# First layer of experts 1 to 6 as seven block products in place of eight, in a chunked-attention and mixture-of-experts kernel

## The chip, the core and the metric

The kernel runs on one core of a Trainium2 chip. Five engines with instruction queues of their own work side by side: TensorE (PE: matmuls, with its weight loads shown apart as PEld), VectorE (DVE), ScalarE (ACT), GpSimd (POOL) and SyncE (SP), from which most DMAs are issued. Each engine takes its instructions strictly in the order in which they stand in its queue; engines wait for each other on semaphores. The metric is the device time of one execution in microseconds, as the median of the runs.

## What is computed

Three stages follow each other; the output of one is the input of the next.

```python
def _moe_ref(x, w_gate, w1, w2):                 # stage 1: x is the attention's output, 1536 x 512
    ...                                          # P: a softmax balanced over tokens and experts, 1536 x 8
    for e in range(E):                           # 8 experts, D = 512, F = 1024
        h = np.maximum(x @ w1[e], 0.0)           # first layer
        ye = h @ w2[e]                           # second layer
        out += P[:, e:e + 1] * ye
    return out

def reference(**kwargs):
    attn_out = _attn_ref(...)                    # 2 x 8 heads, 768 tokens, chunks of 32
    x = attn_out.transpose(0, 2, 1, 3).reshape(B * S, H * D)
    x = _moe_ref(x=x, **moe_kwargs)              # every token through every expert
    return _moe2_ref(x=x, **moe2_kwargs)         # every token through its best expert
```

All is float32. The change concerns `x @ w1[e]` of stage 1 for six of the eight experts.

## The kernel before

Matmuls take operands of 32 bits in a rounded form (F32R). To keep precision each operand is held as two parts, hi (the value rounded) and lo (the rest), and each product is three matmuls into one PSUM accumulation: hi by hi, hi by lo and lo by hi (`mm3`).

The attention's output stands transposed in SBUF as `xhi` and `xlo`: 128 partitions by 4 channel blocks (`KD`) by 1536 tokens. Stage 1 goes through 16 units (expert e, half u of the 1024 hidden columns). A unit goes through groups of four token tiles of 128 (unit 0: of two, because the attention of later tokens still runs). For each group `m1_h` makes four blocks of hidden columns: 12 matmuls of 512 tokens into a PSUM tile `ph`, then ACT writes `hh`, the ReLU rounded, and DVE writes `hl`, the rest. Then `m1_y` makes four tiles of the second layer: 12 matmuls of 512 columns into a PSUM tile `py`, which DVE multiplies by the token's weight and adds to `acc` in SBUF. `ph` and `py` have two buffers each (`ps_m`).

Weights come as chunks of 128 by 512 (256 KB) on SP's queue into four buffers `raw`. `chunk_conv` splits each: ACT casts `raw` to hi (`ah`, `bh`), POOL subtracts to get lo (`al`, `bl`). Eight chunks serve a unit; the table `convs` says after which piece of work each split stands in the program. The order written in the code isn't the order in the queues: the tile framework moves instructions ahead where their inputs allow, by a model of its own.

In unit 1 the attention's PSUM pool (`ps_a`) still serves the balancing of P (`sinkhorn_iter`), of which the steps stand between the matmuls. At its end expert 0's sums are scaled (`scale_expert0`). 36 DMAs (`fills`) that clear buffers of the last stage are taken off a list through the units. In the last unit the routing of stage 2 begins.

```python
nc.scalar.activation(hh, ps, AF.Relu)
nc.vector.scalar_tensor_tensor(hl, ps, 0.0, f32(hh), ALU.max, ALU.subtract)
```

Of the kernel before, what the change touches and what calls it, by code (L numbers as in the profile page):

```python
# [9 lines left out]
F32 = mybir.dt.float32  # L10
F32R = mybir.dt.float32r
# [9 lines left out]
P = 128  # L21
# [6 lines left out]
def f32(ap):  # L28
    return ap.bitcast(F32)
# [3 lines left out]
def kernel(  # L33
# [97 lines left out]
    SK = WN + NM  # L131
    ast = ExitStack()
# [3 lines left out]
    ps_a = ast.enter_context(tc.tile_pool(name="ps_a", bufs=4, space=PSUM))  # L136

# [197 lines left out]

    hcur = {}

    def m1_h(e, u, t0, nt, f):
        ps = ps_m.tile([P, nt * P], F32, tag="ph", name="ph")
        sl = slice(t0 * P, (t0 + nt) * P)  # L340
        fs = slice(f * P, (f + 1) * P)
        terms = []
        for kk in range(KD):
            wh, wl = wts[e, u, "a", kk]
            terms += [(wh[:, fs], xhi[:, kk, sl]), (wh[:, fs], xlo[:, kk, sl]), (wl[:, fs], xhi[:, kk, sl])]
        mm3(ps, terms)
# [391 lines left out]
    post, fills, rq = [], [], []  # L738
    e0 = None
    for nu, (e, u) in enumerate(units):  # L740
        last = nu == len(units) - 1
        gs = [(t, 2) for t in range(0, NT, 2)] if nu == 0 else [(t, GT) for t in range(0, NT, GT)]
        L = sum(NF + nt for _, nt in gs)
        convs = ([13, 15, 16, 25] if nu == 0 else [4, 7, 10, 14]) + [L - 3, L - 2]
        if nu:
            convs += [1, 2]
        if nu == 2:
            zst = ExitStack()
            zrow = zst.enter_context(tc.tile_pool(name="zp", bufs=1, side="right")).tile([P, ROW], F32, name="zrow")
# [32 lines left out]
        for t0, nt in gs:  # L782
# [7 lines left out]
            for wi, w in enumerate(work):  # L790
# [31 lines left out]
        if nu == 1:  # L822
# [110 lines left out]
```

## Time and profile before

| What | Value |
|---|---|
| median of 3 runs | 1349.53 us (1347.64 to 1350.32) |
| profiled execution | 1351.69 us, of which the span from first to last instruction is 1350.0 us |
| mean granted TensorE clock | 0.995 |
| busy in the span | PE 1320.2 us (98%), DVE 506.2, ACT 348.4, POOL 229.6 |
| matmuls | 6604 |

A page of the profile counts an engine as busy from the start of an instruction to its end. Matmuls overlap: the time of one from start to end is longer than the distance to the next, so the pace is read from the starts in the timeline and not from the mean of one. Idle time is put down to the engine that ended it.

### The profile page before, as it was taken

The page shows a single profiled execution, that of the slowest core. Times are in us where ns is not written, and L with a number is a line of the kernel's source. Part 1 is how long each engine was busy: PE and PEld are TensorE (multiplying, and loading weights), DVE is VectorE, ACT ScalarE, POOL GpSimd, SP SyncE. Part 2 cuts the span into 40 slices and gives each one's busy share as a digit, 9 for nine tenths or more (in the row PEclk, how much of TensorE's full clock was granted, in tenths as well). Part 3 has the DMA queues.
Part 4 walks back from the last instruction along what each step waited for, and adds up shares of the span by engine and source line. Part 5 has one row for each costly group of instructions (what it writes and reads, how often), then busy time and mean ns, then how long its engine had stood idle before and what let it go on. Part 6 is the DMA issues. An engine that isn't in the chain of part 4 may idle for free. (4 is left out here: it accounts for less than half of the span.)

```text
span 1350.0 us, 17171 instructions
## 1 busy us (share of the span) xinstructions
PE 1320.2 (98%) x6604; PEld 1093.7 (81%) x6604; DVE 506.2 (37%) x1021; ACT 348.4 (26%) x647; POOL 229.6 (17%) x257
## 2 busy tenths in 40 slices
PE   7999999999999999999999999999999999889997
PEld 6888788888888888888888888888888888678775
DVE  7666353222222222222222222222222234745566
ACT  4332214121202020202121111111111112444455
POOL 5221303030303030303030202021111112300001
PEclk9999999999999999999999999999999999989999
DMA  9342641020202020202020201010111001476560
GB/s 202 88 92 72 187 157 53 10 63 0 63 1 63 0 63 0 63 1 63 0 63 0 63 7 57 16 47 17 46 32 32 0 16 44 159 245 222 167 198 16
DMA packets 86960, 90.86 MB, mean 67 GB/s; under 512 B 49835, under 2 KB 49835, under 8 KB 86852
## 3 DMA queue, kind: packets, MB, share of 16 engines
q1 hardware_dynamic: 84708, 84.15, 21.4%
q0 software_dynamic: 2000, 5.34, 1.1%
q8 instruction: 56, 0.92, 0.3%
q14 instruction: 52, 0.43, 0.1%
q10 hardware_dynamic: 144, 0.03, 0.0%
HBM read 74.70 MB, written 16.03 MB: 67 GB/s over the span
## 5 line engine op out<-in xcount | busy, mean ns | idle before, releaser
L127 PE MATMUL ph<-xhi,ah 128*128 128x512 f32 (+1 forms) x816 | 309.8, 380 | 2.9 <-DVE hl L350 2.9
L127 PE MATMUL ph<-xhi,al 128*128 128x512 f32 (+1 forms) x816 | 308.1, 378 | 0.0
L127 PE MATMUL ph<-xlo,ah 128*128 128x512 f32 (+1 forms) x816 | 307.9, 377 | 0.0
L127 PE MATMUL py<-bh,hh 128*128 128x512 f32 x768 | 300.3, 391 | 0.0
L127 PE MATMUL py<-bl,hh 128*128 128x512 f32 x768 | 299.4, 390 | 0.0
L127 PE MATMUL py<-bh,hl 128*128 128x512 f32 x768 | 299.4, 390 | 0.0
L349 ACT ACTIVATE hh<-ph 128x512 fp32r<-128x512 f32 (+1 forms) x204 | 116.7, 573 | 694.7 <-PE ph L127 681.1
L350 DVE SCALAR_TENSOR_TENSOR hl<-ph,hh 128x512 fp32r<-128x512 f32 (+1 forms) x204 | 134.5, 659 | 378.3 <-ACT hh L349 378.0
L369 DVE SCALAR_TENSOR_TENSOR acc<-py,pr,acc 128x512 f32<-128x512 f32 x168 | 126.2, 751 | 300.2 <-PE py L127 297.2
L119 POOL TENSOR_TENSOR al<-raw,ah 128x512 fp32r<-128x512 f32 x64 | 82.0, 1293 | 741.1 <-ACT ah L118 689.2
L127 PEld LDWEIGHTS ph<-xhi,ah 128*128 128x128 f32 x816 | 153.8, 189 | 31.5 <-DVE hl L350 3.3
L127 PEld LDWEIGHTS ph<-xhi,al 128*128 128x128 f32 x816 | 153.7, 188 | 28.3
L127 PEld LDWEIGHTS ph<-xlo,ah 128*128 128x128 f32 x816 | 153.9, 189 | 27.9
L127 PEld LDWEIGHTS py<-bh,hl 128*128 128x128 f32 x768 | 144.2, 188 | 29.6
L127 PEld LDWEIGHTS py<-bh,hh 128*128 128x128 f32 x768 | 144.2, 188 | 29.4
L127 PEld LDWEIGHTS py<-bl,hh 128*128 128x128 f32 x768 | 144.2, 188 | 29.3
L119 POOL TENSOR_TENSOR bl<-raw,bh 128x512 fp32r<-128x512 f32 x62 | 79.5, 1309 | 53.9 <-ACT bh L118 53.9
L533 DVE TENSOR_TENSOR w<-raw,w 128x512 fp32r<-128x512 f32 x112 | 72.3, 686 | 40.0 <-ACT w L532 39.4
L579 PE MATMUL ph<-w,gx 128*128 128x512 f32 x312 | 80.2, 404 | 1.7 <-PEq L888 1.7
L596 PE MATMUL py<-w,hh 128*128 128x512 f32 x312 | 79.7, 401 | 0.0
L579 PEld LDWEIGHTS ph<-w,gx 128*128 128x128 f32 x312 | 57.9, 191 | 15.8 <-issue 2.9
L532 ACT CAST w<-raw 128x512 fp32r<-128x512 f32 x112 | 63.4, 619 | 9.6 <-DMA raw<-in_moe_w_dram 9.4
(165 smaller groups left out, 769.6 us busy)
## 6 DMA issues: line engine op xcount, KB each, us to landing
raw<-in_moe_w_dram SPq DMA_DIRECT2D x224, 256.0 KB
disp<-zrow SPq DMA_DIRECT2D x24, 257.0 KB
xg<-disp SPq DMA_DIRECT2D x19, 257.0 KB
vin<-in_v_dram SPq DMA_DIRECT2D x20, 176.0 KB
kin<-in_k_dram SPq DMA_DIRECT2D x12, 256.0 KB
qin<-in_q_dram SPq DMA_DIRECT2D x12, 256.0 KB
out_dram<-zrow SPq DMA_DIRECT2D x12, 256.0 KB
vin<-in_mem_v_dram SPq DMA_DIRECT2D x24, 16.0 KB
```

Of the source, the lines that this page charges most:

```text
L119: (eng or nc.gpsimd).tensor_tensor(lo, raw, f32(hi), ALU.subtract)
L127: nc.tensor.matmul(ps, l, r, start=(i == 0), stop=(i == n - 1))
L349: nc.scalar.activation(hh, ps, AF.Relu)
L350: nc.vector.scalar_tensor_tensor(hl, ps, 0.0, f32(hh), ALU.max, ALU.subtract)
L369: nc.vector.scalar_tensor_tensor(a, ps, pr[:, t, e:e + 1], a, ALU.mult, ALU.add)
L532: nc.scalar.copy(h, raw)
L533: nc.vector.tensor_tensor(l, raw, f32(h), ALU.subtract)
L579: nc.tensor.matmul(pss[u], *terms[n], start=(n == 0), stop=(n == len(terms) - 1))
L596: nc.tensor.matmul(py[0], *terms[n], start=(n == 0), stop=(n == len(terms) - 1))
```

## The change

For experts 1 to 6 the units go away. Tokens are cut in two halves of 768 (b=0 and b=1), channels in two halves of 256, hidden columns in two halves of 512. The product of such 2 x 2 blocks takes eight block products; the changed kernel makes seven, of sums and differences of the blocks, and adds the results (the form with 15 additions that is due to Winograd). `m1_g(e, fi, n)` does this for one of four blocks of 128 columns in each half (`fi`) and one of two pieces of 384 tokens in each half (`n`): seven times six matmuls of 384 tokens into four PSUM tiles (`sa`, `sb`, `sc`, `sd`), two of them accumulating a second product, with four additions on DVE, one on POOL and two copies on ACT to combine them through the SBUF tile `stmp`, and four ReLU pairs into slices of `hbig`. `m1_d` then makes six tiles of the second layer (6 matmuls each); they stand one `m1_g` later (`late_d`), and take `ph` and `py` in turn. Each token tile is now added to `acc` four times in an expert, before twice.

The sums of x are made once, in unit 1 (`xs_build`): three go to a new tile `tsum`, one overwrites the upper channel half of the second token half in `xhi` and `xlo`; what stood there is saved to DRAM (`xkeep`) and read back for expert 7. The sums of the weights are made for each `fi` from two chunks of `w1` (`conv_pair`): 11 instructions on POOL and 7 casts on ACT, each on 128 x 256.

```diff
     for e in range(E):
+        if 0 < e < E - 1:
+            wv = w1[e].rearrange("(k p) (u f) -> p k u f", p=P, u=NH)
+            for fi in range(NF):
+                for dh in range(2):
+                    chunks.append((e, fi, "s", dh, wv[:, dh * KH:(dh + 1) * KH, :, fi * P:(fi + 1) * P]))
+                for f in (fi, fi + NF):
+                    chunks.append((e, f // NF, "b", f % NF, w2[e, f * P:(f + 1) * P, :]))
+            continue
...
+    def conv_pair(e, fi):
+        r0, r1 = raw_view(raws.pop(done[0])), raw_view(raws.pop(done[0] + 1))
+        a11, a21, a12, a22 = r0[:, :, 0, :], r0[:, :, 1, :], r1[:, :, 0, :], r1[:, :, 1, :]
+
+        def split(name, x):
+            w = wpa.tile([P, 512], F32R, tag="wa", name="ws").rearrange("p (a k f) -> p a k f", a=2, k=KH)
+            nc.scalar.copy(w[:, 0], x)
+            nc.gpsimd.tensor_tensor(w[:, 1], x, f32(w[:, 0]), ALU.subtract)
+            wts[e, fi, name] = w
+
+        split("a11", a11)
+        split("a12", a12)
+        split("a22", a22)
+        nc.gpsimd.tensor_tensor(a22, a21, a22, ALU.add)
+        split("s1", a22)
+        nc.gpsimd.tensor_tensor(a21, a11, a21, ALU.subtract)
+        nc.gpsimd.tensor_tensor(a11, a22, a11, ALU.subtract)
+        split("s2", a11)
+        split("s3", a21)
+        nc.gpsimd.tensor_tensor(a12, a12, a11, ALU.subtract)
+
+        def rest():
+            split("s4", a12)
+            done[0] += 2
+            chunk_dma(2)
+
+        return rest
...
+        def three(kk, n):
+            (b11, b12, b21, b22), c, _ = parts(kk, n)
+            x11, x12, x22, x21 = [stmp[:, i, :] for i in range(4)]
+            for x, b in ((x11, b11), (x12, b12), (x22, b22), (x21, b21)):
+                nc.gpsimd.tensor_tensor(x, b[0], b[1], ALU.add)
+            nc.gpsimd.tensor_tensor(x11, x12, x11, ALU.subtract)
+            nc.gpsimd.tensor_tensor(x12, x22, x12, ALU.subtract)
+            nc.gpsimd.tensor_tensor(x22, x22, x11, ALU.subtract)
+            nc.gpsimd.tensor_tensor(x21, x22, x21, ALU.subtract)
+            for i, x in ((0, x22), (1, x12), (2, x21)):
+                nc.scalar.copy(tsum[:, i, 0, kk, c], x)
+                nc.vector.tensor_tensor(tsum[:, i, 1, kk, c], x, f32(tsum[:, i, 0, kk, c]), ALU.subtract)
...
+    def m1_g(e, fi, n):
...
+        def put(key, x):
+            z = hcount[1] % 8 * 2 * SN
+            hcount[1] += 1
+            hh, hl = hbig[:, z:z + SN], hbig[:, z + SN:z + 2 * SN]
+            nc.scalar.activation(hh, x, AF.Relu)
+            nc.vector.scalar_tensor_tensor(hl, x, 0.0, f32(hh), ALU.max, ALU.subtract)
+            hsum[fi, n, key] = (hh, hl)
+
+        prod(A, "a11")
+        nc.scalar.copy(s1, A)
+        prod(B_, "s2")
+        nc.vector.tensor_tensor(s1, B_, s1, ALU.add)
+        prod(C, "s1")
+        nc.scalar.copy(s5, C)
+        prod(D_, "a22")
+        prod(A, "a12", True)
+        put((0, 0), A)
+        prod(B_, "s3")
+        nc.vector.tensor_tensor(w, B_, s1, ALU.add)
+        nc.vector.tensor_tensor(c21, w, D_, ALU.subtract)
+        nc.gpsimd.tensor_tensor(s5, w, s5, ALU.add)
+        put((1, 0), c21)
+        prod(C, "s4", True)
+        nc.vector.tensor_tensor(s1, C, s1, ALU.add)
+        put((0, 1), s1)
+        put((1, 1), s5)
...
+        tag = ("py", "ph")[ycount[0] % 2]
...
+            for fi in range(NF):
+                for n in range(NQ):
+                    m1_g(e, fi, n)
+                    if n == 0:
+                        if e < E - 2 or fi < NF - 1:
+                            conv(1)
+                        else:
+                            conv(2)
+                    flush_d()
+                    late_d.append((e, fi, n))
+                    conv(1)
...
+            xq = {2: three[0], 5: three[1], 8: three[2], 11: three[3], 14: one[0], 16: one[1], 18: one[2], 20: one[3]}
```

The first place where the queues differ is ACT at the end of unit 0. Before, after the last cast of the attention (`xhi`), come the ReLU of the unit's last token groups (`hh`, 128 x 256) and the first casts of unit 1's chunks, none of them waiting for POOL:

```order
L285 CAST xhi<-xps 128x4x128 [waits PE_49]
L349 ACTIVATE hh<-ph 128x256 [waits PE_49] x3
L349 ACTIVATE hh<-ph 128x256 [waits PE_49,Activation_49]
L118 CAST ah<-raw 128x512 [waits DMAHW6_49,PE_49]
L118 CAST ah<-raw 128x512 [waits DMAHW7_49,PE_49]
L349 ACTIVATE hh<-ph 128x256 [waits DVE_49,PE_49]
```

Now the casts of `xs_build`, which is written in unit 1, stand there too (`tsum`, each waiting for POOL):

```order
L449 CAST tsum<-stmp 128x384 [waits Pool_49] x5
L405 ACTIVATE hbig<-ph 128x256 [waits PE_49] x2
L449 CAST tsum<-stmp 128x384 [waits Pool_49] x3
L405 ACTIVATE hbig<-ph 128x256 [waits PE_49]
L145 CAST ah<-raw 128x512 [waits PE_49]
L405 ACTIVATE hbig<-ph 128x256 [waits PE_49]
L449 CAST tsum<-stmp 128x384 [waits Pool_49] x3
L145 CAST bh<-raw 128x512 [waits PE_49]
L157 CAST ws<-raw 128x256 [waits DMAHW2_49,DMAHW1_49]
```

What moved: six casts (one more stands ahead of the five shown) that wait for POOL's sums are ahead of the first two of the last four ReLU of unit 0, three more ahead of the third, and three more, with the first casts of a weight pair, ahead of unit 1's first ReLU. POOL's queue at that place, from the first sum on, holds the 32 sums of `three` with no ReLU's work between them.

The second place is ACT in the middle of stage 1. Before, in a unit, 11 ReLU follow each other, and the eight casts of weights stand in one place:

```order
L349 ACTIVATE hh<-ph 128x512 [waits DVE_49,PE_49] x11
L118 CAST ah<-raw 128x512 [waits DMAHW4_49,PE_49]
L118 CAST ah<-raw 128x512 [waits DMAHW5_49,PE_49]
L349 ACTIVATE hh<-ph 128x512 [waits DVE_49,PE_49]
L118 CAST ah<-raw 128x512 [waits DMAHW0_49,Pool_49]
```

Now, in one `m1_g` of every two, the seven casts of the next weight pair (`ws`) are mixed with the copies out of PSUM (`stmp`) and the four ReLU (`hbig`):

```order
L497 COPY stmp<-sa 128x384 [waits DVE_49,PE_49]
L157 CAST ws<-raw 128x256 [waits DMAHW5_49,DMAHW4_49]
L157 CAST ws<-raw 128x256 [waits DMAHW7_49,DMAHW6_49,PE_49]
L501 COPY stmp<-sc 128x384 [waits PE_49]
L157 CAST ws<-raw 128x256
L157 CAST ws<-raw 128x256 [waits PE_49,Pool_49]
L492 ACTIVATE hbig<-sa 128x384 [waits PE_49]
L157 CAST ws<-raw 128x256 [waits Pool_49]
L157 CAST ws<-raw 128x256 [waits PE_49]
L157 CAST ws<-raw 128x256 [waits PE_49,Pool_49]
L492 ACTIVATE hbig<-stmp 128x384 [waits DVE_49]
L492 ACTIVATE hbig<-stmp 128x384 [waits Pool_49]
```

What moved: three of the casts wait for sums that POOL makes in the same stretch, and ReLU stand behind them.

The third place is POOL in that same stretch. Before, its queue held nothing but the subtractions of eight chunks in a unit. Now it holds two of them (`bl`), then ten instructions of a weight pair, and behind these the sum `stmp<-stmp` (L508) of the running `m1_g`, of which the ReLU is the last row above:

```order
L146 TENSOR_TENSOR bl<-raw,bh 128x512 [waits DMAHW1_49,Activation_49]
L146 TENSOR_TENSOR bl<-raw,bh 128x512 [waits DMAHW6_49,Activation_49]
L158 TENSOR_TENSOR ws<-raw,ws 128x256 [waits DMAHW2_49,DMAHW3_49,PE_49,Activation_49]
L158 TENSOR_TENSOR ws<-raw,ws 128x256 [waits DMAHW5_49,DMAHW4_49,Activation_49]
L158 TENSOR_TENSOR ws<-raw,ws 128x256 [waits PE_49,Activation_49]
L164 TENSOR_TENSOR raw<-raw 128x2x128 [waits Pool_49]
L166 TENSOR_TENSOR raw<-raw 128x2x128 [waits Pool_49]
L167 TENSOR_TENSOR raw<-raw 128x2x128 [waits Pool_49]
L158 TENSOR_TENSOR ws<-raw,ws 128x256 [waits Activation_49]
L170 TENSOR_TENSOR raw<-raw 128x2x128 [waits Pool_49]
L158 TENSOR_TENSOR ws<-raw,ws 128x256 [waits PE_49,Activation_49]
L158 TENSOR_TENSOR ws<-raw,ws 128x256 [waits Activation_49]
```

The next row in that queue is L508. What moved: a sum that the second layer needs stands behind twelve instructions that it doesn't need.

## Rows read from the trace of the kernel before

**Rows 1.** The page: span, and busy time of each engine.

```profile
span 1350.0 us, 17171 instructions
PE 1320.2 (98%) x6604; PEld 1093.7 (81%) x6604; DVE 506.2 (37%) x1021; ACT 348.4 (26%) x647; POOL 229.6 (17%) x257
```

**Rows 2.** Windows: busy time of each engine in a unit, then at unit 1's start.

```profile
core 0: us, PE busy (x) PEld busy (x) DVE busy (x) ACT busy (x) POOL busy (x), PEclk, DMA share, GB/s
280.00:345.00 65.00, 65.00 (x289) 53.81 (x288) 17.31 (x24) 12.04 (x20) 10.17 (x8) 1.00 0.11 33
...
166.00:172.00 6.00, 4.43 (x12) 3.42 (x13) 2.55 (x8) 1.65 (x4) 1.74 (x2) 0.72 0.93 295
```

**Rows 3.** Waits of PE from 100 to 1040 us, all of them.

```profile
PE ph L127 <- DVE hl L350: 2.9, 1, 2.9
PE lps L296 <- DVE lt L293: 0.4, 1, 0.4
```

**Rows 4.** Timeline of PE, matmuls of 512: first and 49th of a row of them.

```profile
405.68 0.39 PE L127 MATMUL ph<-xhi,ah 128*128 128x512 f32 x1
...
416.56 0.39 PE L127 MATMUL py<-bh,hh 128*128 128x512 f32 x1
```

**Rows 5.** Timeline of PE, matmuls of 256: first of 22, and what follows them.

```profile
88.10 0.29 PE L127 MATMUL ph<-xhi,al 128*128 128x256 f32 x1
...
90.73 0.40 PE L127 MATMUL py<-bh,hh 128*128 128x512 f32 x1
```

**Rows 6.** Groups by line and form: count, busy us, mean ns, idle before.

```profile
L127 PEld LDWEIGHTS ph<-xhi,ah 128*128 128x128 f32 x816 | 153.8, 189 | 31.5 <-DVE hl L350 3.3
...
L369 DVE SCALAR_TENSOR_TENSOR acc<-py,pr,acc 128x512 f32<-128x512 f32 x168 | 126.2, 751 | 300.2 <-PE py L127 297.2 <-PE lp L441 1.5 <-PE lp L443 1.4
L350 DVE SCALAR_TENSOR_TENSOR hl<-ph,hh 128x512 fp32r<-128x512 f32 x180 | 124.4, 691 | 365.7 <-ACT hh L349 365.6
L349 ACT ACTIVATE hh<-ph 128x512 fp32r<-128x512 f32 x180 | 107.5, 598 | 664.2 <-PE ph L127 650.6 <-PE lp L443 11.2 <-PE cp L473 2.3
L119 POOL TENSOR_TENSOR al<-raw,ah 128x512 fp32r<-128x512 f32 x64 | 82.0, 1293 | 741.1 <-ACT ah L118 689.2 <-PE ph L127 51.9
...
L254 POOL TENSOR_TENSOR es<-es,sm 128x384 f32<-128x384 f32 x24 | 19.8, 827 | 45.5 <-DVE sm L253 41.3 <-DMA vin<-in_v_dram 3.8 <-ACT xhi L285 0.4
...
L350 DVE SCALAR_TENSOR_TENSOR hl<-ph,hh 128x256 fp32r<-128x256 f32 x24 | 10.1, 421 | 12.6 <-ACT hh L349 12.4
...
L349 ACT ACTIVATE hh<-ph 128x256 fp32r<-128x256 f32 x24 | 9.2, 384 | 30.6 <-PE ph L127 30.5
...
L333 ACT ACTIVATE acc<-acc,pr 128x512 f32<-128x512 f32 x12 | 8.1, 719 | 2.6 <-DVE pr L330 1.4 <-DVE acc L367 1.2
...
L430 POOL TENSOR_TENSOR osum<-osum,ohb 128x8 bf16<-128x8 bf16 x11 | 3.7, 333 | 1.4 <-DVE over L451 0.7 <-DVE ohb L424 0.4
```

**Rows 7.** Timeline of POOL at 25 us, and of DVE in the same stretch.

```profile
25.04 3.48 POOL L119 TENSOR_TENSOR bl<-raw,bh 128x512 fp32r<-128x512 f32 x2 [1.33 <-ACT bh L118]
...
23.49 0.76 DVE L119 TENSOR_TENSOR bl<-raw,bh 128x512 fp32r<-128x512 f32 x1
...
25.59 1.79 DVE L119 TENSOR_TENSOR bl<-raw,bh 128x512 fp32r<-128x512 f32 x1
```

**Rows 8.** Timeline of POOL at the end of unit 0.

```profile
142.26 0.53 POOL L750 MEMSET zrow<- 128x514 f32 x1 [4.97 <-PE glp L127]
```

**Rows 9.** Timeline of ACT, last ReLU of unit 0 and first of unit 1.

```profile
149.34 0.38 ACT L349 ACTIVATE hh<-ph 128x256 fp32r<-128x256 f32 x1 [7.90 <-PE ph L127]
...
164.26 0.62 ACT L118 CAST bh<-raw 128x512 fp32r<-128x512 f32 x1 [2.53 <-DMA raw<-in_moe_w_dram]
...
166.20 1.08 ACT L349 ACTIVATE hh<-ph 128x512 fp32r<-128x512 f32 x2
```

**Rows 10.** Timeline of SP's queue there.

```profile
161.57 4.08 SPq L106 DMA_DIRECT2D raw<-in_moe_w_dram  x4
```

**Rows 11.** Timeline of DVE in a unit: second layer's add, then `hl`.

```profile
405.88 0.75 DVE L369 SCALAR_TENSOR_TENSOR acc<-py,pr,acc 128x512 f32<-128x512 f32 x1 [1.97 <-PE py L127]
409.23 0.69 DVE L350 SCALAR_TENSOR_TENSOR hl<-ph,hh 128x512 fp32r<-128x512 f32 x1 [2.60 <-ACT hh L349]
```

**Rows 12.** All instructions on tile `raw`: minimum, median and maximum ns.

```profile
L119 POOL TENSOR_TENSOR bl<-raw,bh x62: 1282/1294/1788, 25.0 to 1080.4; 128x512 fp32r<-128x512 f32 x62
```

More of the change, by code (lines that the diff above doesn't have):

```diff
@@ new lines, in m1_g, with prod @@
+    def m1_g(e, fi, n):
+        c = slice(n * SN, (n + 1) * SN)
+        c2 = slice(S + n * SN, S + (n + 1) * SN)
+        top, low = slice(0, KH), slice(KH, KD)
+        xin = {
+            "a11": (xhi[:, top, c], xlo[:, top, c]),
+            "a12": (xhi[:, low, c], xlo[:, low, c]),
+            "s4": (xhi[:, low, c2], xlo[:, low, c2]),
+            "a22": (tsum[:, 2, 0, :, c], tsum[:, 2, 1, :, c]),
+            "s1": (xhi[:, top, c2], xlo[:, top, c2]),
+            "s2": (tsum[:, 0, 0, :, c], tsum[:, 0, 1, :, c]),
+            "s3": (tsum[:, 1, 0, :, c], tsum[:, 1, 1, :, c]),
+        }
+        A, B_, C, D_ = [ps_s.tile([P, SN], F32, tag="s" + x, name="s" + x) for x in "abcd"]
+        s1, s5, w, c21 = [stmp[:, i, :] for i in range(4)]
+        def prod(ps, name, more=False):
+            wt, (xh, xl) = wts[e, fi, name], xin[name]
+            terms = []
+            for kk in range(KH):
+                terms += [(wt[:, 0, kk], xh[:, kk]), (wt[:, 0, kk], xl[:, kk]), (wt[:, 1, kk], xh[:, kk])]
+            for i, (l, r) in enumerate(terms):
+                nc.tensor.matmul(ps, l, r, start=(i == 0 and not more), stop=(i == len(terms) - 1), skip_group_check=more)
+        def put(key, x):
[23 more added lines that the diff above has]
+        put((1, 1), s5)
@@ new lines, with m1_d @@
+    ycount = [0]
+    def m1_d(e, fi, n, half, i):
+        t = half * TPB + n * SQ + i
+        ycount[0] += 1
+        tag = ("py", "ph")[ycount[0] % 2]
+        ps = ps_m.tile([P, 512], F32, tag=tag, name=tag)
+        ts_ = slice(i * P, (i + 1) * P)
+        terms = []
+        for g in range(2):
+            hh, hl = hsum[fi, n, (g, half)]
+            wh, wl = wts[e, g, "b", fi]
+            terms += [(hh[:, ts_], wh), (hh[:, ts_], wl), (hl[:, ts_], wh)]
+        mm3(ps, terms)
+        a = acc[:, t, 0:DM]
+        nc.vector.scalar_tensor_tensor(a, ps, pr[:, t, e:e + 1], a, ALU.mult, ALU.add)
@@ L738, with flush_d @@
     post, fills, rq = [], [], []
-    e0 = None
+    xkeep = dramp.tile([P, 2, KH, S], F32, name="xkeep")
+    late_d = []
+    def flush_d():
+        while late_d:
+            e_, fi_, n_ = late_d.pop(0)
+            for half in range(2):
+                for i in range(SQ):
+                    m1_d(e_, fi_, n_, half, i)
     for nu, (e, u) in enumerate(units):
         last = nu == len(units) - 1
-        gs = [(t, 2) for t in range(0, NT, 2)] if nu == 0 else [(t, GT) for t in range(0, NT, GT)]
+        if 0 < e < E - 1:
+            if u:
+                continue
+            if nu == 2:
+                ps_s = sst.enter_context(tc.tile_pool(name="ps_s", bufs=1, space=PSUM))
+                zst = ExitStack()
+                zrow = zst.enter_context(tc.tile_pool(name="zp", bufs=1, side="right")).tile([P, ROW], F32, name="zrow")
+                nc.gpsimd.memset(zrow, 0.0)
+                nc.gpsimd.memset(zrow[:, DM:DM + 1], BIG)
+                fills = fill_list(zrow)
+                conv(1)
[5 more added lines that the diff above has]
+                            conv(1)
+                        else:
+                            conv(2)
+                    flush_d()
+                    late_d.append((e, fi, n))
+                    conv(1)
+                    if fills:
+                        fills.pop(0)()
+            if e == E - 2:
+                for i, z in enumerate((xhi, xlo)):
+                    nc.sync.dma_start(f32(z[:, 0:KH, S:N]), xkeep[:, i])
+                flush_d()
+                conv(1)
+                for f in fills:
+                    f()
+                zst.close()
+                sst.close()
+            continue
+        gs = [(t, 2) for t in range(0, NT, 2)] if nu == 0 else [(t, GT) for t in range(0, NT, GT)]
+        if nu == 1:
+            gs = gs[::-1]
+            for i, z in enumerate((xhi, xlo)):
+                nc.sync.dma_start(xkeep[:, i], f32(z[:, 0:KH, S:N]))
+            ast.close()
+            sst = ExitStack()
+            spool = sst.enter_context(tc.tile_pool(name="spool", bufs=1, side="right"))
+            tsum = spool.tile([P, 3, 2, KH, S], F32R, name="tsum")
+            stmp = spool.tile([P, 4, SN], F32, name="stmp")
+            three, one = xs_build()
+            xq = {2: three[0], 5: three[1], 8: three[2], 11: three[3], 14: one[0], 16: one[1], 18: one[2], 20: one[3]}
```

86 lines of the change are left out of this document (60 added, 26 removed).

## Prediction

> **What bounds the kernel now.** I read the page's busy line first, then stretches by window, then PE's waits, then timelines. The reader is to see that PE is busy for 98% of the span [rows 1], that in a unit of stage 1 it is busy for all 65 of 65 us while DVE has 17, ACT 12 and POOL 10 [rows 2], and that from 100 to 1040 us it waits twice, for 2.9 and 0.4 us [rows 3]. So a matmul saved in stage 1 is time saved, and any new wait of PE is time lost. The 2.9 us stand at the start of unit 1, with a mean granted clock of 0.72 (some of that stretch at 1.2 GHz in place of 2.4) in the six us after it [rows 2, 3]: the one place where PE already depends on others.
>
> **The saving.** The pace is read from starts. 48 matmuls of 512 take 416.56 - 405.68 = 10.88 us, 0.2267 each [rows 4]; 22 of 256 take 90.73 - 88.10 = 2.63 us, 0.1195 each [rows 5]. That is 0.0124 us fixed and 0.1071 for 256 columns; for 384 it gives 0.173. An expert's first layer had 288 matmuls of 512, 65.3 us; it has now 4 x 2 x 7 x 6 = 336 of 384, 58.1 to 58.3 us. The second layer keeps 288 of 512. Saved: 7.05 us an expert, **42.3 us** over six.
>
> **POOL's prices.** Everything else hangs on POOL. Its two-operand instruction takes 1.293 us on 512 columns, 0.827 on 384 where one operand is one value for many columns, and 0.333 on 8 [rows 6]. On 256, half of 1.293 gives 0.65 and the line through 8 and 512 gives 0.80: I take 0.72, the middle. On 384, 0.827 is the lower bound and the line's 1.05 the upper; I take three quarters of 1.293, 0.97, since both operands are full here. ACT on 384 lies between 0.384 and 0.598: 0.49; `hl` on DVE between 0.421 and 0.691: 0.56; an add to `acc` 0.751 [rows 6]. A hand-over is about 0.06 us.
>
> **End of unit 0.** The framework has moved `xs_build` to where the attention's buffers come free, so POOL begins at 142.3 [rows 8] on 32 sums, and ACT's casts, which wait for them, stand ahead of ReLU. The first ReLU of the last group ran at 149.34 [rows 9]; now 16 sums are ahead of it: 142.3 + 16 x 0.97 + 1 + 0.5 = 159. PE's two `ph` buffers are full by then, so it waits. The first ReLU of unit 1 ran at 166.20 [rows 9]. Ahead of it are now 34 sums (two of `one` too), two subtractions of chunks, about 1.5 us of POOL's waits on itself and on DVE, then the DMA of the next raw pair, which needs the buffer that POOL frees last (from issue at 161.57 to use at 164.26 it takes 2.7 [rows 9, 10]), and two casts of 0.38: 142.3 + 33.0 + 2.6 + 1.5 + 2.7 + 0.8 = 182.9, **16.7 us** later; 12 with sums of 0.827. SP clears buffers and saves `xkeep` in the same stretch, but POOL is later than both. Unit 1 has no slack to win this back, PE being always busy in it. For the clock I add 2 us (0 to 4): 28% of six us once or twice more [rows 2].
>
> **Port.** At 25 us a POOL pair of subtractions took 3.48 where two take 2.6, one of them 1.788, while DVE did the same operation, both operands in SBUF, in 1.79 in place of 0.76 [rows 6, 7, 12]: each loses about 1 us of an overlap. In a unit DVE's `hl` has one operand in PSUM, and nobody loses [rows 6, 11]. The change gives DVE operations with two SBUF operands: 12 of 384 in `three`, and three `hl` of each `m1_g`. The Trainium skill (GPSIMD Engine Reference, Specifications) says that POOL shares its SBUF interface with VectorE and that they collide for DVE instructions with two SBUF inputs; by it each such overlap would cost in full, the second rival below, and the rows at 25 us agree with it, on one occasion. I take half: 12 x 0.75 / 2 = 4.5 us at unit 0's end, which makes **21** (12 to 27).
>
> **Each weight pair.** One `m1_g` of two carries the splits of the next pair. Let the tile of second layer before it end at 0. PE then needs 42 x 0.173 = 7.3 us for the seven products and 24 x 0.2267 = 5.44 for four tiles of second layer, and at **12.7** it wants a PSUM buffer back: the first add to `acc` must be done. DVE comes to that add only after the last `hl`, that after the last ReLU, that (ACT being in order) after the ReLU of the POOL sum, and this sum stands behind two `bl` and ten instructions on 256. Two `bl` end at 2.7 (they wait for the buffers that the tile just ended frees); ten by 0.72 with five hand-overs and a wait for ACT 10.3; the sum on 384 11.3; two ReLU 12.3; `hl` 12.9; the add 13.7 or, with hand-overs, **13.8**. PE waits 1.1 us, and this once for each pair. Of 24 pairs two are made before the stretch is regular: 22 times. With 0.65 the chain ends 0.9 earlier, at 12.9; with the line's 0.80 and 1.05 it ends at 14.7. A collision adds up to 0.75 us on POOL ahead of its sum and some on the `hl` behind it; I take 0.4. So 1.5 us x 22 = **33** (4 to 48, the upper end being 2.2 each). ACT's and DVE's own time does not bind: in the 30.9 us of two `m1_g` with their tiles DVE has about 18, ACT about 10, POOL about 12. In the other `m1_g` POOL has only its sum and the ReLU come in time.
>
> **Small terms.** Entering expert 1: ACT still scales expert 0 (12 x 0.719 [rows 6]) between the first casts and copies; 3 us (0 to 5). Reading `xkeep` back is 1.6 MB under 8 us of late tiles and the first four-tile group of expert 7, some 21 us; without that cover it would cost under 10. The `fills` wait for nothing; more adds to `acc` are in DVE's 18 us. More and smaller weight DMAs move the same 4 MB per expert, and have a pair's 31 us to land.
>
> **Sum:** -42.3 + 21 + 2 + 33 + 3 = **+17 us** on the profiled 1351.7. The median is 2.2 us below it: 1349.5 + 17 = 1366.
>
> **Rivals.**
> *POOL is quick enough (faster).* If ten instructions on 256 take 0.61 us or less and nothing collides, the add is done by 12.7 and PE never waits: -42.3 + 12 + 0 + 0 to 5 = -30 to -25, 1320 to 1325. Half waits give up to 1346. For it: 0.65 is nearly there, and the collision was seen once. Against: an instruction has some fixed cost, 0.333 on 8 columns. The point from which it decides: with unit 0's end at 21 and 5 for the small terms, 42.3 is reached at a wait of 0.74 us a pair, a chain that ends at 13.4.
> *Every overlap collides.* Then -42.3 + 27 + 4 + 5 + 48 = +42, 1391. The rule above and the rows at 25 us speak for it; that `hl` and POOL must just meet speaks against.
> *No collision, middle prices.* -42.3 + 17 + 2 + 24 + 3 = +4, 1353: the edge of the likeliest case.
> *Weight loads set the pace*, so that the change does not save what it counts: a load shows 0.189 us [rows 6]; were that the pace, 336 would take 63.5 us, saving only 1.8 an expert: +48, 1398. Against it: matmuls of 256 go at 0.12 with the same loads [rows 5].
> The Trainium skill (GPSIMD Engine Reference, Engine selection) advises VectorE for two-operand elementwise work, POOL being about twice slower; DVE's 0.76 against POOL's 1.293 on one form agrees [rows 6, 7]. It speaks against giving POOL the sums, and changes no term.
>
> **How the numbers follow.** Likeliest, 0.40: slower by 3 to 33 us, 1353 to 1382, with 1366 in it. All collide or worse: 0.18. Loads bind: 0.02. Balance within 0.2% (about what a measurement of this kernel can tell from no change, 2.7 us): 0.08. Faster: 0.32. So slower 0.60. The range leaves a tenth out at each end: 1324 to 1391.
>
> **What would show it.** Right: 384-column matmuls 0.173 apart; a PE wait of 7 to 12 us near 150 behind ReLU, with ACT's `tsum` casts waiting for POOL; then 22 waits of 1 to 2 us on the second layer's `ph`, by the add to `acc`, 31 to 33 us apart; `hl` from `stmp` longer than 0.56. Wrong: POOL's 256 columns under 0.62, no waits on `ph`, or 384-column matmuls at 0.19.

## The result, and the profile after

| | before | changed |
|---|---|---|
| median of 4 runs | 1349.92 us (1347.64 to 1351.54) | 1366.65 us (1366.11 to 1369.2) |
| ratio | | 1.0129, 95% interval 1.0109 to 1.0148 |
| profiled execution, its span | 1351.69, 1350.0 | 1369.2, 1367.4 |
| mean granted TensorE clock | 0.995 | 0.989 |

The page of the changed kernel, span and busy times, to be held against [rows 1]: PE is busy for less (1301.5 us for 1320.2) in a longer span, DVE for 44% more and POOL for nearly twice as long.

```profile
span 1367.4 us, 18950 instructions
PE 1301.5 (95%) x6892; PEld 1128.5 (83%) x6892; DVE 728.5 (53%) x1429; ACT 435.2 (32%) x927; POOL 451.2 (33%) x557
```

Waits of PE in the changed kernel (us in total, times, longest), the first three. Between 100 and 1040 us there were two short ones before [rows 3]:

```profile
PE ph L182 <- DVE acc L530: 21.3, 22, 1.5
PE py L182 <- ACT hbig L405: 11.9, 2, 9.8
PE ph L182 <- DVE hbig L406: 8.0, 3, 6.3
```

To see where the 17 us arise, the stage is cut at three points that both timelines have: the matmul in unit 1 that waits for the unit's first ReLU (its 25th; the 24 ahead of it need none), the first of expert 1, the first of expert 7. PE's timeline, changed kernel:

```profile
188.90 0.79 PE L182 MATMUL ph<-xhi,ah 128*128 128x512 f32 x1 [6.26 <-DVE hbig L406]
...
254.87 0.33 PE L486 MATMUL sa<-xhi,ws 128*128 128x384 f32 x1
...
1032.16 0.39 PE L182 MATMUL ph<-xhi,ah 128*128 128x512 f32 x1
```

and before:

```profile
167.57 0.50 PE L127 MATMUL ph<-xhi,ah 128*128 128x512 f32 x1 [2.93 <-DVE hl L350]
...
231.60 0.39 PE L127 MATMUL ph<-xhi,ah 128*128 128x512 f32 x1
...
1014.96 0.39 PE L127 MATMUL ph<-xhi,ah 128*128 128x512 f32 x1
```

Expert 1 begins 23.3 us later (21.3 of them are there at unit 1's wait). The six experts then take 777.3 us in place of 783.4, a gain of 6.1 where 42.3 was counted on, so expert 7 begins 17.2 us later, and nothing changes that behind it (the spans differ by 17.4). The cut is used for every experiment below. Points ahead of expert 1 can be compared between traces to 2 us only: five experiments run code that is the same, or all but the same, up to there, and their expert 1 begins at 252.6 to 253.1, in this trace at 254.9. A length such as 777.3 repeats better: experiments 9 and 10, less the rows that they add, have 777.0 and 776.9.

**One weight pair.** The first m1_g of a pair begins at 523.13. POOL, then ACT, then DVE, at its end:

```profile
531.33 0.75 POOL L170 TENSOR_TENSOR raw<-raw 128x256 f32<-128x256 f32 x1
532.03 1.45 POOL L158 TENSOR_TENSOR ws<-raw,ws 128x256 fp32r<-128x256 f32 x2
533.44 1.33 POOL L508 TENSOR_TENSOR stmp<-stmp 128x384 f32<-128x384 f32 x1
```

```profile
532.11 0.41 ACT L157 CAST ws<-raw 128x256 fp32r<-128x256 f32 x1 [0.81 <-POOL raw L170]
532.42 0.52 ACT L492 ACTIVATE hbig<-stmp 128x384 fp32r<-128x384 f32 x1
534.80 0.94 ACT L492 ACTIVATE hbig<-stmp 128x384 fp32r<-128x384 f32 x2 [1.86 <-POOL stmp L508]
```

```profile
532.98 0.92 DVE L493 SCALAR_TENSOR_TENSOR hbig<-stmp,hbig 128x384 fp32r<-128x384 f32 x1 [1.12 <-ACT hbig L492]
535.36 1.03 DVE L493 SCALAR_TENSOR_TENSOR hbig<-stmp,hbig 128x384 fp32r<-128x384 f32 x2 [1.46 <-ACT hbig L492]
536.30 0.75 DVE L530 SCALAR_TENSOR_TENSOR acc<-ph,pr,acc 128x512 f32<-128x512 f32 x1
```

PE, the same place one pair earlier and in this one:

```profile
503.35 0.39 PE L182 MATMUL py<-bh,hbig 128*128 128x512 f32 x1
504.68 0.50 PE L182 MATMUL ph<-bh,hbig 128*128 128x512 f32 x1 [0.94 <-DVE acc L530]
505.01 0.39 PE L182 MATMUL ph<-bl,hbig 128*128 128x512 f32 x1
...
507.55 0.33 PE L486 MATMUL sa<-xhi,ws 128*128 128x384 f32 x1
...
514.93 0.39 PE L182 MATMUL ph<-bh,hbig 128*128 128x512 f32 x1
...
523.13 0.33 PE L486 MATMUL sa<-xhi,ws 128*128 128x384 f32 x1
...
537.10 0.50 PE L182 MATMUL ph<-bh,hbig 128*128 128x512 f32 x1 [0.94 <-DVE acc L530]
```

Read against the engine's order: the sum L508 ends 11.6 us after the start, the first add to acc 13.9, and PE goes on at 13.97. The starts show more than the wait of 0.94: from 503.35 to 504.68 are 1.33 where 0.227 is the pace, and the next start comes 0.33 later, not 0.227. So a pair loses 1.1 + 0.1 = **1.2 us**, and 22 pairs 27. POOL and DVE meet once in it, and take turns: hl, begun at 532.98, took 0.92 us in place of 0.55 and ended 0.42 after POOL's L158 (533.90 and 533.48); L508, begun at 533.44, took 1.33 in place of 1.02 and ended 0.87 after hl.

**End of unit 0.** ACT there, and PE's first matmul behind the wait:

```profile
158.25 0.51 ACT L449 CAST tsum<-stmp 128x384 fp32r<-128x384 f32 x1 [6.26 <-POOL stmp L445]
...
161.01 0.65 ACT L405 ACTIVATE hbig<-ph 128x256 fp32r<-128x256 f32 x2
...
177.25 0.52 ACT L449 CAST tsum<-stmp 128x384 fp32r<-128x384 f32 x1 [6.17 <-POOL stmp L445]
...
186.92 0.71 ACT L157 CAST ws<-raw 128x256 fp32r<-128x256 f32 x2 [4.89 <-DMA raw<-in_moe_w_dram]
187.54 0.59 ACT L405 ACTIVATE hbig<-ph 128x512 fp32r<-128x512 f32 x1
```

```profile
161.44 0.80 PE L182 MATMUL py<-bh,hbig 128*128 128x512 f32 x1 [9.83 <-ACT hbig L405]
```

ACT's casts wait for POOL's sums, and the ReLU that stood at 149.34 and 166.20 [rows 9] now run at 161.01 and 187.54.

### The profile page after: what moved, and what is told of

Same layout as the page of the kernel before. It is cut to its first block, busy times and chain, and to the rows that moved or that the text cites. A ratio compares the mean times of both kernels' runs of the same rounds, so it can differ in the third digit from the quotient of the medians.

```text
span 1367.4 us, 18950 instructions
## 1 busy us (share of the span) xinstructions
PE 1301.5 (95%) x6892; PEld 1128.5 (83%) x6892; DVE 728.5 (53%) x1429; ACT 435.2 (32%) x927; POOL 451.2 (33%) x557
## 5 line engine op out<-in xcount | busy, mean ns | idle before, releaser
L182 PE MATMUL py<-bh,hbig 128*128 128x512 f32 x960 | 328.0, 394 | 12.4 <-ACT hbig L405 11.9
L182 PE MATMUL ph<-bh,hbig 128*128 128x512 f32 x576 | 204.3, 395 | 21.3 <-DVE acc L530 21.3
L182 PEld LDWEIGHTS py<-bh,hbig 128*128 128x128 f32 x960 | 180.8, 189 | 51.1 <-ACT hbig L405 12.6
L182 PE MATMUL py<-bl,hbig 128*128 128x512 f32 x480 | 188.4, 392 | 0.0
L508 POOL TENSOR_TENSOR stmp<-stmp 128x384 f32<-128x384 f32 x48 | 55.8, 1163 | 272.5 <-DVE stmp L506 272.4
L158 POOL TENSOR_TENSOR ws<-raw,ws 128x256 fp32r<-128x256 f32 x168 | 123.0, 746 | 52.0 <-ACT ws L157 50.7
L530 DVE SCALAR_TENSOR_TENSOR acc<-py,pr,acc 128x512 f32<-128x512 f32 x144 | 107.6, 748 | 42.1 <-PE py L182 42.0
L486 PE MATMUL sb<-tsum,ws 128*128 128x384 f32 x576 | 117.5, 340 | 0.0
L530 DVE SCALAR_TENSOR_TENSOR acc<-ph,pr,acc 128x512 f32<-128x512 f32 x144 | 107.6, 747 | 17.2 <-PE ph L182 16.4
L486 PE MATMUL sa<-xhi,ws 128*128 128x384 f32 x384 | 114.2, 338 | 0.0
L486 PE MATMUL sc<-xhi,ws 128*128 128x384 f32 x384 | 113.4, 336 | 0.6 <-ACT stmp L501 0.6
L182 PE MATMUL ph<-bl,hbig 128*128 128x512 f32 x288 | 112.9, 392 | 0.0
L182 PE MATMUL ph<-xhi,ah 128*128 128x512 f32 (+1 forms) x240 | 86.9, 363 | 8.0 <-DVE hbig L406 8.0
```

What stands on the lines that cost most here:

```text
L158: nc.gpsimd.tensor_tensor(w[:, 1], x, f32(w[:, 0]), ALU.subtract)
L182: nc.tensor.matmul(ps, l, r, start=(i == 0), stop=(i == n - 1))
L486: nc.tensor.matmul(ps, l, r, start=(i == 0 and not more), stop=(i == len(terms) - 1), skip_group_check=more)
L508: nc.gpsimd.tensor_tensor(s5, w, s5, ALU.add)
```

## The experiments

Ratios are to the kernel before, run beside on the same chip, where its median was 1349.5 to 1352.7 us; the changed kernel's is 1.0129. "Stretch" is from expert 1's first matmul to expert 7's: 783.4 us before, 777.3 changed. The forecasts in us start from the changed kernel's 1366.6, so a run beside a slower before is held against them by its ratio: experiment 1 then stands at 1352, 2 at 1342, 3 at 1389 and 4 at 1350.

**1. POOL's sum of m1_g to DVE.**

```diff
-        nc.gpsimd.tensor_tensor(s5, w, s5, ALU.add)
+        nc.vector.tensor_tensor(s5, w, s5, ALU.add)
```

> The one sum of an m1_g that POOL makes (L508) goes to DVE; nothing else changes. Theory P (POOL's queue): this sum is late because it stands behind twelve instructions, and the ReLU behind it holds DVE's adds to acc. In the trace after, the 22 waits show 0.94 us each (21.3 in all) and the period of a weight pair loses 1.22 us with the slow restart. Then all 22 waits on L530 go, 22 x 1.22 = 27 us: 1366.6 - 27 = 1340 (1336 to 1346), and DVE's sum takes about 0.56 us, up to 0.92 beside POOL. Rival A (ACT's queue): the ReLU are late because casts of ws, which wait for POOL's sums of weights, stand ahead of them; these stay, so most of the waits stay, at least 16 of 22: 1355 to 1366. Rival C: the waits are a by-product of PE's pace and come back elsewhere: 1362 to 1368.

Measured: 1354.8 us, ratio 1.0022 (1.0011 to 1.0032), stretch 763.8. All 22 waits are still there, at a third of their length:

```profile
PE ph L182 <- DVE acc L530: 7.5, 22, 0.9
```

Neither theory's number: all 22 waits stay, as rival A has it, but two thirds of their length went with POOL's sum, and something else kept the rest alive. The groups by form of this run name a candidate: the three hl that read stmp take 0.695 us each, where the one that reads PSUM takes 0.557, and POOL's L170, beside DVE's sums, takes 1.10 where L167 ahead of it has 0.74. The 0.695 is a mean of two kinds: from the first regular pair on, the 89 that met no instruction of POOL took 0.55 us each, the 40 that came while one ran 1.00 on average, and each of these ended 0.41 to 0.42 us after POOL's instruction, however early it had begun.

```profile
L493 DVE SCALAR_TENSOR_TENSOR hbig<-stmp,hbig 128x384 fp32r<-128x384 f32 x144 | 92.6, 695 | 22.8 <-ACT hbig L492 22.8
L493 DVE SCALAR_TENSOR_TENSOR hbig<-sa,hbig 128x384 fp32r<-128x384 f32 x48 | 26.7, 557 | 160.7 <-ACT hbig L492 160.7
L170 POOL TENSOR_TENSOR raw<-raw 128x256 f32<-128x256 f32 x24 | 26.3, 1096 | 1.8
L167 POOL TENSOR_TENSOR raw<-raw 128x256 f32<-128x256 f32 x24 | 17.7, 736 | 1.9
```

**2. The four sums of weights to DVE** (in `conv_pair`, four lines alike):

```diff
-        nc.gpsimd.tensor_tensor(a22, a21, a22, ALU.add)
+        nc.vector.tensor_tensor(a22, a21, a22, ALU.add)
```

> The four sums of weights in conv_pair go from POOL to DVE; L508 stays on POOL. Theories P and A agree here: POOL's chain gets shorter by four instructions of 0.74 us with a hand-over each (about 3.1 us), more than the 1.22 us that a pair loses, and the casts behind these sums come earlier; the waits on L530 go, 1340 (1336 to 1347). Rival D (DVE's queue): DVE now waits for POOL's subtractions before it may overwrite the chunk, and what stands behind, the copies out of PSUM, is late: waits of PE on sb or sa in place of those on ph, 1350 to 1370.

Measured: 1344.3 us, ratio 0.9943 (0.9927 to 0.9960), stretch 748.9; no wait on L530 is left, and none on sa or sb in its place. At unit 1's start DVE's sums, which wait for POOL, stand ahead of hl, and PE waits longer there:

```profile
191.40 0.80 PE L182 MATMUL ph<-xhi,ah 128*128 128x512 f32 x1 [12.24 <-DVE hbig L406]
```

Expert 1 begins at 258.5 in place of 254.9, which is why the whole gained 25 us and the stretch 28.

**3. One more instruction on POOL.**

```diff
         split("s2", a11)
+        nc.gpsimd.tensor_tensor(wts[e, fi, "s2"][:, 1], a11, f32(wts[e, fi, "s2"][:, 0]), ALU.subtract)
```

> One of POOL's subtractions in conv_pair (the low part of s2) is made twice, so POOL has one more instruction of 128 x 256 ahead of L508 in each pair; the result is the same. Theory P: the chain of each of the 22 pairs gets longer by one such instruction, 0.74 us, and PE's wait by as much: 22 x 0.74 = 16 us, 1383 (1379 to 1388), waits of about 1.7 us. Rival C (the waits don't depend on POOL): no change, 1364 to 1369.

Measured: 1391.37 us, ratio 1.0294 (1.0272 to 1.0316), stretch 801.9, 24.6 more. The waits grow by 0.82 each (39.3 - 21.3 over 22), as theory P has it, C falls. But 24.6 is more than 22 x 0.82 = 18. Of the 21 waits behind expert 1's first pair, 1.76 us each, three stand in pairs that took 34.8 us where the others took 33.2, and in these three the granted clock fell behind a wait as long as the others'; it also fell behind the first of the 22 waits, the longest with 2.28. These four make up the rest. The window of the first wait, and of one of the three:

```profile
276.00:286.00 10.00, 9.08 (x39) 8.14 (x40) 4.89 (x8) 0.96 (x2) 0.00 (x0) 0.83 0.14 38
...
546.00:556.00 10.00, 10.00 (x45) 9.03 (x46) 3.88 (x6) 1.14 (x3) 0.00 (x0) 0.83 0.05 17
```

(The 0.83 is the clock.) From 546.96 to 549.95 the starts there are 0.43 apart, which is 1.2 GHz, and 0.227 before and after.

**4. The sums of x held back to unit 1.** A copy on DVE of a few columns of what unit 1's latest step wrote goes ahead of the sums, and another ahead of their casts, three or four steps later; the table `xq` spreads the parts over unit 1 anew:

```diff
+            nc.vector.tensor_copy(stmp[:, :, 0], late[0])
             for x, b in ((x11, b11), (x12, b12), (x22, b22), (x21, b21)):
...
+            nc.vector.tensor_copy(tsum[:, :, 0, kk, n * SN], late[0][:, 0:3])
             for i, x in ((0, x22), (1, x12), (2, x21)):
```

> The sums of xs_build stay on POOL and their casts on ACT, but a copy of four columns on DVE, which reads what the unit's latest step wrote, keeps them from starting ahead of their place in unit 1; the casts of each are held back in the same way until about four steps after its sums. Theory B1 (ACT's queue at the end of unit 0): the ReLU were late because casts that wait for POOL stood ahead of them; PE's waits of 9.8, 0.4, 2.1, 0.5, 6.3 and 1.3 us (20.4) between 150 and 196 us shrink to the 2.9 that the kernel before has, with 2 to 4 us of slower clock and restarts, and unit 1 hides the 36 sums: 1366.6 - 20 = 1347 (1343 to 1352). Rival B2 (the DMAs that save xkeep and clear buffers): unit 1's first ReLU stays late, only the 13 us at the end of unit 0 come back: 1354 to 1358. Rival B3 (unit 1 has no room for 36 sums): the waits move to unit 1 and the start of expert 1: 1358 or more.

Measured: 1353.57 us, ratio 1.0007 (0.9995 to 1.0019). PE's wait in unit 1 is 0.76 us, and expert 1 begins at 233.25, 1.7 us after the kernel before in place of 23.3 (to the 2 us named above):

```profile
164.06 0.50 PE L182 MATMUL ph<-xhi,ah 128*128 128x512 f32 x1 [0.76 <-DVE hbig L406]
...
233.25 0.33 PE L494 MATMUL sa<-xhi,ws 128*128 128x384 f32 x1
```

So B1 holds and B2 falls: the DMAs that save xkeep and clear buffers still run from 139 us on. 4.8 us come back at the start of expert 1 (stretch 782.1), in two waits of 1.2 and 2.8 us where ACT waits for a chunk of weights ahead of its copies: a little of B3.

**5. Experiment 1 without two SBUF operands in hl.**

```diff
-        nc.vector.tensor_tensor(c21, w, D_, ALU.subtract)
-        nc.gpsimd.tensor_tensor(s5, w, s5, ALU.add)
-        put((1, 0), c21)
+        nc.vector.tensor_tensor(D_, w, D_, ALU.subtract)
+        nc.vector.tensor_tensor(B_, w, s5, ALU.add)
+        put((1, 0), D_)
...
-        nc.vector.tensor_tensor(s1, C, s1, ALU.add)
-        put((0, 1), s1)
-        put((1, 1), s5)
+        nc.vector.tensor_tensor(C, C, s1, ALU.add)
+        put((0, 1), C)
+        put((1, 1), B_)
```

> As e1_s5dve, and the results of the three combining operations (c21, s5, s1) are written over PSUM tiles (sd, sb, sc) in place of stmp, so that hl of these three reads PSUM and not two operands in SBUF. In e1_s5dve the 22 waits shrank from 0.94 to 0.34 us but stayed; there the three hl took 2.40 us together and POOL's L170, beside DVE's sums, 1.12 in place of 0.74. Theory S (the port): what kept the wait alive is DVE's operations with two SBUF operands meeting POOL's; hl then takes about 0.5 to 0.56 each, the chain ends 0.7 us earlier, the 22 waits go: stage 1's seven-product stretch 763.8 - 12 = 752 us (749 to 755), ratio to before 1.0022 - 0.009 = 0.993 (0.990 to 0.996). Rival Q (three operations in a row on DVE simply take that long): hl keeps 0.8 us, the waits stay at 0.3, ratio 1.001 to 1.003. Rival R: the PSUM tiles are held longer and PE waits for them (sb, sc, sd) in the next m1_g: ratio above 1.003.

Measured: ratio 0.9936 (0.9915 to 0.9958), 1340.83 us, stretch 750.5; of the 22 waits on L530 one is left, 0.9 us, in expert 1's first pair. The three hl take 0.55 each, with the same work beside them on POOL:

```profile
L493 DVE SCALAR_TENSOR_TENSOR hbig<-sd,hbig 128x384 fp32r<-128x384 f32 x48 | 26.5, 552 | 21.8 <-ACT hbig L492 21.8
L493 DVE SCALAR_TENSOR_TENSOR hbig<-sc,hbig 128x384 fp32r<-128x384 f32 x48 | 26.3, 547 | 0.0
L493 DVE SCALAR_TENSOR_TENSOR hbig<-sb,hbig 128x384 fp32r<-128x384 f32 x48 | 26.3, 547 | 0.0
```

Theory S holds for hl: what experiment 1 left was the price of DVE's two SBUF operands beside POOL, and rival Q falls, since hl has the same length in both runs where POOL is away. Rival A of experiment 1 falls with it, since ACT's casts of ws wait for POOL's sums here as they did there. L170 still takes 1.13 us in a pair: the sum on DVE that begins just ahead of it has two SBUF operands as before, and here POOL is the second. The Trainium skill (GPSIMD Engine Reference, Specifications) says that POOL's SBUF interface is shared with VectorE and contended when a DVE instruction has two SBUF inputs; by that the loss goes with the second SBUF operand, and 0.695 against 0.55 us agrees.

**6 to 8. Both mended.** Experiment 2 with 4; the same with expert 1's first pair left on POOL; experiment 5 with 4.

> e2_wsumdve and e4_gate2p together. The seven-product stretch took 748.9 us in e2 (777.3 after the change), and expert 1 began at 233.3 us in e4 (254.9 after the change). If the two terms are independent, both gains add up, less some 5 us of waits at the start of expert 1 that e4 showed: ratio to before 1.0129 - 0.0186 - 0.0122 - 0.0027 = 0.979 (0.977 to 0.984). Rival: DVE's sums for expert 1's first pair, which wait for POOL, stand ahead of unit 1's hl (in e2 PE waited 12.2 us there) and keep unit 1 late by 5 to 12 us: 0.984 to 0.990.

> As e6_sums_gate_a, but the sums of expert 1's first weight pair stay on POOL, so that no DVE sum that waits for POOL stands ahead of unit 1's hl. Independent terms: 0.979 (0.976 to 0.983), and better than e6_sums_gate_a by 5 us or more if the rival named there holds, the same within 2 us if not.

> e5_psum and e4_gate2p together; all sums of weights stay on POOL. Expert 1 began at 233.3 us in e4 and the seven-product stretch took 750.5 us in e5; with about 5 us of waits at the start of expert 1, as in e4, e6 and e7, expert 7 would begin at 989 us (989.3 in e7) and the ratio to before be 0.981 (0.978 to 0.984). If the port matters at the start of expert 1 as well, where DVE's and POOL's sums meet, it is a little better than e7: 0.978. If the two gains hinder each other, 0.985 or more.

Measured: 1326.95 us, ratio 0.9831 (0.9811 to 0.9851); 1324.57, 0.9815 (0.9789 to 0.9840); 1328.06 beside a before of 1352.7, 0.9818 (0.9801 to 0.9834). The two gains add up (1.0129 - 0.0186 - 0.0122 = 0.982), and the three versions can't be told apart: expert 7 begins at 990.2, 989.3 and 988.6 us, where it began at 1014.96 before. The rival of the first (DVE's sums ahead of hl cost 5 to 12 us) falls: unit 1's first wait is 2.6 us there. All three beat both kernels, the one before by 1.7 to 1.9%, with intervals that end below 1.

**9 and 10. The pace of 384 columns.** Rows of 24 matmuls more behind expert 6, read by nobody:

```diff
+                for n, m in ((384, 24), (384, 6), (256, 24), (320, 24), (448, 24), (512, 24)):
+                    for i in range(24):
+                        if i % m == 0:
+                            pt = ps_m.tile([P, 512], F32, tag="ph", name="pt")
+                        nc.tensor.matmul(pt[:, 0:n], (bh, bl)[i % 2][:, i % 4 * P:(i % 4 + 1) * P], xhi[:, 2 + i // 2 % 2, 0:n], start=(i % m == 0), stop=(i % m == m - 1))
```

> The changed kernel with 144 more matmuls after expert 6, whose products nobody reads: six rows of 24, each matmul with weights of its own, of 384 columns (one accumulation of 24), 384 (accumulations of 6), 256, 320, 448 and 512. It measures the pace on which the saving rests. Theory L (a straight line between 256 and 512 columns, 0.0124 us plus 0.000418 a column): 0.173 for 384, 0.146 for 320, 0.200 for 448. In the trace after the change 42 matmuls of 384 took 7.38 us, 0.1757 each. Rival G (a change of accumulation or PSUM tile costs): 0.173 in one accumulation of 24, 0.176 in accumulations of 6. Rival O (384 columns just aren't on the line): 0.1755 to 0.177 in both rows. The time as a whole: 1366.6 + 25 = 1392.

> As e8_pace, with seven rows of 24 matmuls of 384 in accumulations of six, to find why the block products run at 0.1757 us a matmul where e8_pace had 0.1733 for 384 on the line: in turn a control as in e8 (weights bh and bl in turn, xhi from token 0), the kernel's own pattern (weights ws; xhi, xlo, xhi; tokens from 384), the same with xhi alone from token 0, the control from token 384, the control with a weight used twice in a row, the control with xhi and xlo in turn, and the kernel's own pattern again. Theory K (the operands): the kernel's pattern shows 0.1755 or more both times, and one of the other rows shows which part of it does. Rival N (other engines at work beside): every row runs at 0.1733, within 0.0005, once the adds after expert 6 have ended, and the 0.0024 come from what ACT, DVE and POOL do beside the block products.

Measured, in the first (1391.28 us), where each row of 24 begins:

```profile
1029.60 0.33 PE L945 MATMUL pt<-xhi,bh 128*128 128x384 f32 x1
...
1033.79 0.33 PE L945 MATMUL pt<-xhi,bh 128*128 128x384 f32 x1
...
1037.95 0.28 PE L945 MATMUL pt<-xhi,bh 128*128 128x256 f32 x1
...
1040.81 0.31 PE L945 MATMUL pt<-xhi,bh 128*128 128x320 f32 x1
...
1044.34 0.36 PE L945 MATMUL pt<-xhi,bh 128*128 128x448 f32 x1
...
1049.20 0.39 PE L945 MATMUL pt<-xhi,bh 128*128 128x512 f32 x1
```

By 24: 0.1746 and 0.1733 for 384, 0.119 for 256, 0.147 for 320, 0.2025 for 448. The line holds (448 is 1% above it); a change of accumulation costs nothing, so G and O fall. In the second (1396.36 us) seven rows of other kinds, 168 matmuls with the kernel's own pattern among them, begin at 1029.97, and expert 7 follows at 1059.11: 0.1734 each. So none of these kinds is slow; but no row reads `tsum`, as three of the seven products do. Where the block products lose time shows in the starts of one m1_g of the changed kernel, the one from 507.55 to 514.93 above, here from its second product on:

```profile
508.61 1.22 PE L486 MATMUL sb<-tsum,ws 128*128 128x384 f32 x6
509.67 0.34 PE L486 MATMUL sc<-xhi,ws 128*128 128x384 f32 x1
...
510.72 1.22 PE L486 MATMUL sd<-tsum,ws 128*128 128x384 f32 x6
511.78 0.34 PE L486 MATMUL sa<-xhi,ws 128*128 128x384 f32 x1
...
512.82 1.22 PE L486 MATMUL sb<-tsum,ws 128*128 128x384 f32 x6
513.88 0.34 PE L486 MATMUL sc<-xhi,ws 128*128 128x384 f32 x1
```

Six matmuls at 0.1733 are 1.04 us. The first product takes 1.06, the three with `tsum` 1.06 each, the three behind these 1.04 to 1.05. The first product's loss comes with the change from 512 to 384 columns: the first six matmuls of the first row of experiment 9, also behind 512 columns, take 1.07 with no block product beside them. That other engines' work is the cause (rival N) is not borne out: every m1_g from the third on takes 7.38 to 7.39 us, and also in experiments 5 and 8, where POOL makes no sum in it. With a weight pair ACT has five casts more in these 7.4 us, POOL has no pause, and the ReLU of sa, which falls into the last product with `tsum`, begins 0.66 us later (6.14 us after the start, else 5.48); yet the 42 starts stand where they stand without. K stands as far as `tsum` goes; what it is in `tsum` that costs 0.02 us a product was not tested.

## Why the prediction was right

**The result** of 1366.65 lies on the forecast of 1366, and partly by luck: two terms were off by 5 and 6 us in opposite directions.

**The saving**, counted as 42.3: the pace from the line, 0.173, is that of long rows (0.1733). In m1_g it is 7.38 / 42 = 0.1757 us. 336 of them are 59.0 us, so 6.2 us an expert and **37.4** over six. The term was 5 us too large because a pace of long rows of one kind was used for 42 matmuls that begin behind others of 512 columns and read `tsum` in three products of seven. [rows 4] were themselves taken while ACT, DVE and POOL worked.

**POOL's prices**: 0.74 us on 256 columns (0.72 was taken), 1.01 on 384 (0.97), ACT's ReLU on 384 0.49 to 0.52 (0.49), hl 0.56 without a collision (0.56).

**End of unit 0**, 21 and 2 for the clock: 23.3 measured at expert 1. The first ReLU ran at 161.0 (159 was forecast, without the port) and unit 1's at 187.5 (182.9 and 4.5 for the port). That the second falls on the forecast is partly chance: POOL began 1 us later and a sum took 1.01 for 0.97, while the port cost POOL less than 4.5 (next paragraph). Experiment 4 took the delay away by moving where the sums and casts stand, with every one of them still made.

**Port**, half of the overlaps: the mechanism is simpler than the half. Where two instructions meet that both read two operands in SBUF, the first loses nothing and the second waits for it: hl and the low parts of tsum end 0.41 to 0.42 us after the instruction of POOL that they met, all 36 times in the changed kernel, and L508 0.87 to 0.88 after hl, 22 times. So an overlap costs in full, to the one that came second. DVE's low parts of tsum took 1.09 us in the changed kernel and 0.62 in experiment 4, where POOL's sums for the next part wait until they are done. POOL's sums lost less, some 2.4 us over the 32 of `three` (the 16 of L443 took 1.14 each for 1.02 in experiment 4, the four of L447 1.15 for 1.04), where 4.5 was taken. In m1_g it is the collision that keeps a third of the wait (experiments 1 and 5): L508 takes 1.33 us in the pairs, 1.02 in the other m1_g, and 1.01 in the pairs of experiment 3, where POOL came to it after hl was done. So 0.3 us a pair, where 0.4 was taken.

**Each weight pair**, 22 times 1.5 = 33: 22 waits came, at the place and in the order of the chain (sum at 11.6 for 11.3 forecast, add done at 13.9 for 13.8 without and 14.2 with a collision). They show 0.94 us and cost 1.2 with the restart, so **27**.

**Small terms**, 3: what is left of the stretch, 777.3 - (783.4 - 37.4 + 27), is 4.3. About 2 of it are second layer: its 36 matmuls behind each m1_g take 523.13 - 514.93 = 8.20 us, by the pace of [rows 4] 8.16. Most of the rest stands in expert 1's first pair, where PE waits 1.5 us on L530 and 0.6 on ACT's copy.

So -37.4 + 23.3 + 27 + 4.3 = 17.2, as the cut at expert 7 shows.

**The rivals.** "POOL is quick enough" needed 0.61 us on 256 columns, and POOL has 0.74. Its 1320 to 1325 was too low even for a kernel without the waits: experiments 2 and 5 stand at 0.994 of before, some 1341, since the saving is 37 and the end of unit 0 costs 23, not 12. "Every overlap collides" (1391): every overlap does collide, but a pair has one, of one hl of three with POOL, and a wait cost 1.2 us, not 2.2. "No collision" would have been 1353: no experiment tests it alone, since experiment 5 removes the collision of hl and also POOL's place in the chain. "Weight loads set the pace" falls: a load shows 0.188 us ahead of 384 columns too, and they go at 0.173 to 0.176.

## What to carry to other kernels

Fewer matmuls pay only if the work that feeds and joins them is on time in the order of the queues: here 37 us of matmuls were bought with 50 us lost to waits on engines that were busy for about half the time or less. Look in each in-order queue for an early instruction that waits on a slow engine and has urgent work behind it; moving its place, or one to four instructions to another engine, gave 14 to 25 us without taking any work away. A scheduler that starts work as soon as its inputs allow may put it ahead of what is urgent; a small dependency on the step that it should follow holds it back.

## What the runs showed of the hardware that was not expected

- A wait of PE costs more than it shows: 0.94 us shown, 1.2 lost, since the matmul before it ends later than its pace and the first behind it takes 0.33 to the next start in place of 0.227.
- Of 21 waits of 1.76 us three were followed by some 3 us at 1.2 GHz, which cost 1.5 us each; with waits of 0.94 us none of the pairs showed it. What tells the three apart from the other 18 is open.
- DVE and POOL take turns where both read two operands in SBUF: of two instructions that meet, the second ends a fixed time after the first, 0.41 to 0.42 us for DVE's on 384 columns, 0.87 to 0.88 for POOL's sum L508, 0.59 to 0.61 for POOL's on 256 (the changed kernel, experiments 1, 2, 3 and 5). With one operand in PSUM hl took 0.55 us with POOL beside it as without.
- Matmuls of 384 columns went at 0.1733 us in long rows and at 0.1757 in the block products. The loss comes behind a change from 512 columns and in products that read `tsum`, and repeats to 0.01 us whatever the other engines do; why is open.
